# v loaded as fp32 by SyncE's queue and cast on chip, and every engine's order given as a list

## The chip, the cores and the metric

The kernel runs on one core of one Trainium2 chip. A core has five engines that work side by side and meet through semaphores: TensorE (PE, matrix products), VectorE (DVE), ScalarE (ACT), GpSimd (POOL) and SyncE (SP, which here only issues DMAs). Each takes its own instructions strictly in the order in which they were written. The metric is the time on the device in microseconds (us), as the median of some runs; less is better.

## The reference

Two layers follow one another. The first is causal attention with a choice of key chunks: 4 batches, 8 heads, 768 positions, 64 dimensions, 24 chunks of 32 keys. The second is an FFN over the 3072 rows of 512 that attention gives.

```python
k_min, k_max = min and max of k over each chunk of 32 keys
ub = sum over d of maximum(q * k_min, q * k_max)      # an upper bound per query and chunk
top_chunks = the 6 chunks with the largest ub among the causal ones
scores = q @ k.T / 8, masked to the chosen chunks and to keys not after the query
attn = softmax(scores) @ v

rms = sqrt(mean(x * x) + 1e-6);  xn = x / rms * rms_g
out = (silu(xn @ w_gate) * (xn @ w_val)) @ w_out       # 512 -> 1536 -> 512
```

## The kernel before

**Tiling.** Attention goes by pairs of heads: 4 batches of 4 pairs, 16 pairs (p0 to p15), each with 768 positions in 6 tiles of 128. The steps of a pair, by the names that the code gives them: `kload`, `qload` (DMAs into buffers of the kind `nat`, 7 of them, 2 heads side by side); `kT`, `qT` (fp32 transposes on PE, three tiles a step) and `kE`, `qE` (their evictions from PSUM); `kmx`, `kmn`, `dif` (chunk maxima, minima, difference); `kC`, `qC` or `qN` (casts to bf16); `relu`, `ub`, `ubE`, `up`, `ubm` (the bounds: matmul, eviction, transpose, causal mask; for p6 and later two pairs at once, in `duo`); `max`, `sel` (the sixth largest bound and the 0/1 choice), which go to PE's operand through `selT` and `selC` for p0 to p2 and through a DMA transpose on SP (`qX`) from p3 on; `sc`, `exp`, `mask`, `av` (scores, exponential, diagonal mask from batch 1 on, product with v), 6 groups for each of two heads (p3 is worked in two halves of three query tiles); and `xb` (division by the sum).

v of a pair (step `v`, function `load_v`, line 477) is one DMA on GpSimd's queue. It reads fp32 rows of 64 from DRAM and writes bf16 into one of four buffers VX, of 12 x 65 elements a partition, whose column 64 holds ones, set at the start, so that `av` also gives the sum of the exponentials.

The FFN goes by half batches of 384 rows (f0.0 to f3.1). A norm n of the same name comes ahead of each: three `sq` (sums of squares), `eps`, `root`, three `xs` (scaled rows), then a transpose on PE (`tp`, `tpE`) for batch 0 or by DMA on SP (`xT`) later. Then 12 times `gate`, `tanh`, `tg`, `val`, `hh`, and for each of three row tiles three `po` (products with w_out), `poE` (eviction) and `out` (DMA on SP). The weights come as six DMAs of 768 KB on GpSimd's queue (`wg`, `wv`, `wo`).

**Order.** The code first adds all steps to a list, each with its dependencies, the buffers that it opens and uses, the engines that may take it and a planned duration; class `Order` (line 79) then puts them in order. `run` plays the program forward: whenever an engine is free it takes, of the steps that are ready and find buffers, the one with the lowest rank. The ranks are sums of the numbers in `RANK` and `TIMES`. `LIMITS` keeps the 8 PSUM banks apart: so many for scores, preparation, FFN and so on. The steps are then emitted by their planned start. The engine of a step with several choices is the one that takes it first.

**Fillers.** Step `busy` is a matmul on zeros into a free PSUM bank: 48 of 512 columns, free from the start, and 40 of 256 columns, free after the last scores of p2. Their rank is 1000 and more, so the planner takes one only where PE has nothing else.

The lines that the sections below speak of: 346 (filler), 481 (v load), 505 (k and q load), 525 (`kT`, `qT`), 297 to 303 (function `evict`: evictions and casts, whatever the step), 565 (`qX`), 876 (`sc`), 893 (`exp`), 912 (`av`), 932 and 933 (`xb`), 960 and 963 (`sq`), 989 (`xs`), 1045 (`gate`), 1052 (`tanh`), 1058 (`tg`), 1066 (`val`), 1074 (`hh`), 1086 (`po`), 1101 (`out`).

Of the kernel before, what the change touches and what calls it, by code (L numbers as in the profile page):

```python
# [8 lines left out]
FP32 = mybir.dt.float32  # L9
# [16 lines left out]
RANK = (  # L26
    dict(
        av=439.71, dif=-349.0, eps=-276.35, exp=56.9, kC=119.11, kE=221.89, kT=-479.5,
        kload=-91.99, kmn=-561.73, kmx=-221.73, max=-117.69, qC=120.39, qE=644.67, qN=97.14,
        qT=303.27, qX=110.23, qload=17.43, relu=-156.64, root=392.56, sc=392.96, sel=176.91,  # L30
        selC=388.0, selT=-168.59, sq=-325.5, tp=-47.15, tpE=460.17, ub=-387.44, ubE=-1000.64,
        ubm=-238.37, up=-379.03, vload=-360.06, xb=-167.37, xs=293.02,
    ),
    dict(
        av=-243.01, dif=-122.81, eps=-968.41, exp=80.0, gate=-57.45, hh=-33.27, kC=474.21,
        kE=54.78, kT=-28.02, kload=327.35, kmn=571.37, kmx=673.95, mask=-6.85, max=351.72,
        out=-338.93, po=268.25, poE=188.61, qE=-4.14, qN=444.8, qT=271.57, qX=-691.62,
        qload=314.07, relu=202.91, root=-1348.37, sc=-186.72, sel=354.08, sq=285.76, tanh=579.3,
        tg=-259.04, ub=-101.04, ubE=-390.25, ubm=307.49, up=-117.99, val=-52.48, vload=103.56,
        xT=119.23, xb=-299.83, xs=-84.52,  # L40
    ),
)

TIMES = {
# [34 lines left out]
class Order:  # L79
# [18 lines left out]
    def run(self, places):  # L98
        import heapq
        for s in self.steps:  # L100
            s.rank = sum(places[k] * x for k, x in s.keys.items())
            for d in s.deps:
                d.next.append(s)
            s.left = len(s.deps)
        free = {e: 0.0 for e in ("PE", "ACT", "DVE", "POOL", "SP")}
        held = {k: [None] * n for k, n in self.slots.items()}
        count = {}
        waiting = {e: [] for e in free}
        dma = port = 0.0
        n = 0  # L110
        for s in self.steps:
            s.n = n
            n += 1
            if not s.left:
                for e in s.engs:
                    waiting[e].append(s)
        events = [0.0]
        out = []
        while len(out) < len(self.steps):
            if not events:  # L120
                stuck = [x for e in waiting for x in waiting[e] if x.start is None]
                raise RuntimeError("no step can go: " + ", ".join(x.name for x in stuck[:20]))
            t = heapq.heappop(events)
            while events and events[0] <= t + 1e-9:
                heapq.heappop(events)
            for e in free:
                if free[e] > t + 1e-9:
                    continue
                best = None
                for s in waiting[e]:  # L130
                    if s.start is not None or s.ready > t + 1e-9:
                        continue
                    if best is not None and (s.rank, s.n) >= (best.rank, best.n):
                        continue
                    if s.load > 250000 and dma > t + 3.0:
                        heapq.heappush(events, dma - 3.0)
                        continue
                    ok, want = True, {}
                    for b in s.opens:
                        if b.slot is not None:  # L140
                            continue
                        if b.sub and count.get(b.sub, 0) + want.get(b.sub, 0) >= self.limits(b.sub, t):
                            ok = False
                        got = sum(h is None or (h.users == 0 and h.done <= t + 1e-9)
                                  for h in held[b.kind])
                        want[b.kind] = want.get(b.kind, 0) + 1
                        if b.sub:
                            want[b.sub] = want.get(b.sub, 0) + 1
                        if got < want[b.kind]:
                            ok = False  # L150
                    if ok:
                        best = s
                if best is None:
                    continue
                s = best
                s.start, s.eng = t, e
                occ = s.occ[e]
                if e == "PE" and t < self.COLD:
                    occ = 2 * occ

                if e == "DVE" and s.port:
                    occ = max(free["POOL"] - t, 0.0) + occ
                    port = t + occ
                elif e == "POOL":
                    occ = max(port - t, 0.0) + occ
                s.seen = t + occ + self.TAIL[e]
                if s.load:
                    dma = max(dma, t + occ) + s.load / self.RATE
                    s.seen = dma + 1.5
                free[e] = t + occ  # L170
                heapq.heappush(events, free[e])
                heapq.heappush(events, s.seen)
                for b in s.opens:
                    if b.slot is None:

                        b.slot = min((i for i, h in enumerate(held[b.kind])
                                      if h is None or (h.users == 0 and h.done <= t + 1e-9)),
                                     key=lambda i: held[b.kind][i].done if held[b.kind][i] else -1.0)
                        held[b.kind][b.slot] = b
                        if b.sub:  # L180
                            count[b.sub] = count.get(b.sub, 0) + 1
                for b in s.bufs:
                    b.users -= 1
                    b.done = max(b.done, s.seen)
                    if b.users == 0 and b.sub:
                        count[b.sub] -= 1
                for x in s.next:
                    x.left -= 1
                    x.ready = max(x.ready, s.seen)
                    if not x.left:  # L190
                        for y in x.engs:
                            waiting[y].append(x)
                        heapq.heappush(events, x.ready)
                for y in s.engs:
                    waiting[y].remove(s)
                out.append(s)
        self.span = max(s.seen for s in out)
        return out
# [3 lines left out]
def kernel(  # L202
# [11 lines left out]
    nc = tc.nc  # L214
# [22 lines left out]

# [921 lines left out]
```

## Time and profile before

| | us |
|---|---|
| median of 3 runs (315.83 to 316.9) | 315.89 |
| span of the profiled execution | 314.0 |
| PE busy | 308.6 (98%) |
| DVE busy | 230.7 (73%) |
| ACT busy | 194.4 (62%) |
| POOL busy | 100.7 (32%) |

The profiled execution's own time is its span, from the first to the last instruction; the median lies 1.9 us above it. Times in rows are us from the span's start. A row of a group reads: line, engine, operation, output <- input with shapes, count | busy us, mean ns of one | idle time ahead, and what ended it. A row of a window reads: the stretch, its length, busy us and count of instructions of each engine, granted clock of PE, share of the DMA engines, GB/s. A row of a wait reads: who, for whom: us in total, times, longest. A row of the timeline reads: start, duration, engine, line, what, count, and in brackets the idle time ahead. Busy time of PE runs from the first start to the modelled end of pipelined matmuls, so PE can be busy throughout and still have room.

### The profile page before, as it was taken

To read this page: it belongs to the slowest core of one execution; us is meant where nothing else is said; L and a number is where in the kernel's file an instruction comes from. 1 tells how busy PE (TensorE), PEld (TensorE's weight loads), DVE (VectorE), ACT (ScalarE), POOL (GpSimd) and SP (SyncE) were. 2 spreads that over 40 slices of the span, in tenths; PEclk is the share of its full clock that TensorE was granted. 3 is DMA by queue.
4 is the path that set the end of the run, shared out by engine and by line. 5 is a ranking of instruction groups with operands and counts; after the bars stand their busy time and mean duration, and the time that the engine had idled before them with its cause. 6 is when DMAs were issued, how large, how long until landed. Compare 5 with 4: busy or idle time off the path is not lost.

```text
span 314.0 us, 7640 instructions
## 1 busy us (share of the span) xinstructions
PE 308.6 (98%) x2844; PEld 196.1 (62%) x2844; DVE 230.7 (73%) x654; ACT 194.4 (62%) x420; POOL 100.7 (32%) x157
## 2 busy tenths in 40 slices
PE   7999999999999999999999999999999999999995
PEld 4567877666566775666667565656666645655542
DVE  7699986888988487967986799879464663873530
ACT  5589987863475987478579654344988823333321
POOL 8666534342353564045357300001522220000000
PEclk9999999999999999999999999999999999999999
DMA  8999989989989898979934640002341045001102
GB/s 171 210 190 178 145 108 207 198 114 143 196 86 199 126 179 152 201 164 222 158 79 61 93 102 0 2 2 52 84 94 59 20 118 150 3 0 65 38 22 111
DMA packets 113301, 35.36 MB, mean 113 GB/s; under 512 B 106224, under 2 KB 110064, under 8 KB 113264
## 3 DMA queue, kind: packets, MB, share of 16 engines
q1 hardware_dynamic: 83152, 26.62, 40.9%
q0 software_dynamic: 28512, 7.87, 25.6%
q10 hardware_dynamic: 1600, 0.39, 0.6%
q8 instruction: 22, 0.36, 0.5%
q14 instruction: 15, 0.12, 0.1%
HBM read 28.57 MB, written 6.29 MB: 111 GB/s over the span
## 4 chain that ended last, share of the span: by engine, by line
PE 97%; DMA 1%; ACTq 0%; ACT 0%; issue 0%
PE gp L1045 20%; PE vp L1066 20%; PE po L1086 20%; PE sc L876 12%; PE av L912 7%; PE busy L346 4%; PE pq L525 4%; PE pk L525 3%; PE ub L789 2%; PE ub L731 2%; DMA qnat<-in_q_dram 1%; PE up L811 1%; PE sc L882 1%; PE up L755 1%; PE tp L1011 0%; ACTq L505 0%
## 5 line engine op out<-in xcount | busy, mean ns | idle before, releaser
L893 ACT ACTIVATE pt<-sc 128x512 bf16<-128x512 f32 (+2 forms) x192 | 88.4, 578 | 10.1 <-PE sc L876 5.3
L1052 ACT ACTIVATE sg<-gp 128x384 bf16<-128x384 f32 x96 | 47.7, 500 | 62.7 <-PE gp L1045 60.0
L1066 PE MATMUL vp<-xT,wv 128*128 128x384 bf16 x384 | 77.0, 326 | 0.0
L1045 PE MATMUL gp<-xT,wg 128*128 128x384 bf16 x384 | 76.2, 326 | 0.0
L1086 PE MATMUL po<-wo,hh 128*128 128x512 bf16 x288 | 69.3, 379 | 0.0
L1058 DVE SCALAR_TENSOR_TENSOR tg<-sg,gp 128x384 bf16<-128x384 bf16 x96 | 52.2, 548 | 21.7 <-ACT sg L1052 19.5
L1074 DVE TENSOR_TENSOR hh<-vp,tg 128x384 bf16<-128x384 f32 x96 | 51.8, 551 | 11.1 <-PE vp L1066 7.3
L1045 PEld LDWEIGHTS <-wg 128*128 128x128 bf16 x384 | 36.8, 98 | 24.5 <-issue 1.0
L1066 PEld LDWEIGHTS <-wv 128*128 128x128 bf16 x384 | 36.9, 98 | 24.1
L876 PE MATMUL sc<-qs,ke 128*128 128x128 bf16 (+5 forms) x420 | 51.4, 251 | 0.0
L1086 PEld LDWEIGHTS <-hh 128*128 128x128 bf16 x288 | 27.6, 98 | 27.5
L301 POOL CAST ke<-kt 64x768 bf16<-64x768 f32 x31 | 26.4, 852 | 36.9 <-ACT kt L297 17.0
L876 PEld LDWEIGHTS <-ke 128*128 128x128 bf16 (+1 forms) x420 | 30.3, 97 | 11.3 <-issue 1.6
L899 POOL TENSOR_SCALAR_AFFINE_SELECT pt<-pt 128x512 bf16<-128x512 bf16 (+1 forms) x48 | 24.4, 527 | 37.6 <-ACT pt L893 37.4
L912 PEld LDWEIGHTS <-pt 128*128 128x128 bf16 x672 | 28.8, 98 | 7.7 <-POOL ke L301 0.6
L912 PE MATMUL av<-vx,pt 128*128 128x65 bf16 x672 | 32.6, 193 | 0.0
L299 ACT ACTIVATE osb<-po 128x512 f32<-128x512 f32 x19 | 11.4, 602 | 21.4 <-PE po L1086 21.4
L346 PE MATMUL busy<-zeros 128*128 128x512 bf16 (+1 forms) x88 | 20.1, 349 | 1.3 <-DVE zeros L341 1.3
L933 DVE TENSOR_TENSOR xb<-av,rden 128x384 bf16<-128x384 f32 (+1 forms) x34 | 18.1, 534 | 1.2
L989 DVE SCALAR_TENSOR_TENSOR xs<-xb,ri,gains 128x512 bf16<-128x512 bf16 x24 | 16.9, 746 | 2.7 <-DMA xT<-xs 2.1
L301 POOL CAST qn<-qnat 128x768 bf16<-128x768 f32 x10 | 8.2, 821 | 31.9 <-DMA qs<-qn 30.7
L481 POOL DMA_DIRECT2D vx<-in_v_dram x16 | 16.8, 1052 | 4.0 <-PE av L912 2.6
(87 smaller groups left out, 303.1 us busy)
## 6 DMA issues: line engine op xcount, KB each, us to landing
out_dram<-osb SPq DMA_DIRECT2D x24, 256.0 KB, 2.2
knat<-in_k_dram SPq DMA_DIRECT2D x30, 192.0 KB, 4.3
qnat<-in_q_dram SPq DMA_DIRECT2D x30, 192.0 KB, 4.8
vx<-in_v_dram POOLq DMA_DIRECT2D x16, 192.0 KB, 4.7
wg<-in_moe_w_gate_dram POOLq DMA_DIRECT2D x2, 768.0 KB, 8.6
wv<-in_moe_w_val_dram POOLq DMA_DIRECT2D x2, 768.0 KB, 7.8
wo<-in_moe_w_out_dram POOLq DMA_DIRECT2D x2, 768.0 KB, 9.9
qs<-qn SPq DMA_TRANSPOSE x26, 3.3
```

The source lines that it names most:

```text
L301: engine[e].tensor_copy(out_, in_)
L346: nc.tensor.matmul(t[:, 0:n], zeros[:, 0:P], zeros[:, 0:n], start=True, stop=True)
L876: nc.tensor.matmul(t[:, x:x + m, :].rearrange("p a b -> p (a b)"), ke[kk, kb * P:(kb + 1) * P], qs[kk, q0 * P:(q0 + m) * P], start=not tri ...
L893: nc.scalar.activation(out=t[:, 0:nn, :], in_=sc.tile[:, 0:nn, :], func=ACT.Exp, scale=SCALE)
L899: nc.gpsimd.affine_select(out=pt.tile[:, 0:nd, :], in_=pt.tile[:, 0:nd, :], compare_op=ALU.is_ge, fill=0.0, base=0, pattern=[[0, nd], [1, ...
L912: nc.tensor.matmul(av.tile[:, qi - i0, :], pt.tile[:, x, :], VX[c.v.slot][:, hl * NT + kb, :], start=(begin and m == 0), stop=(left[0] == ...
L1045: nc.tensor.matmul(t[:], wg[:, g, hs], XT[b].tile[:, g, cols], start=(g == 0), stop=(g == NP - 1))
L1052: nc.scalar.activation(out=t[:], in_=gp.tile[:], func=ACT.Tanh, scale=0.5)
L1058: nc.vector.scalar_tensor_tensor(out=t[:], in0=sg.tile[:], scalar=1.0, in1=gp.tile[:], op0=ALU.add, op1=ALU.mult)
L1066: nc.tensor.matmul(t[:], wv[:, g, hs], XT[b].tile[:, g, cols], start=(g == 0), stop=(g == NP - 1))
L1074: nc.vector.tensor_tensor(out=t[:], in0=vp.tile[:], in1=tg.tile[:], op=ALU.mult)
L1086: nc.tensor.matmul(po.tile[:], hhs[ht].tile[:, th * P:(th + 1) * P], wo[:, ht, :], start=(ht == 0), stop=(ht == NHT - 1))
```

## The change

1. `VDIRECT = range(16)`: for every pair, `load_v` now makes two steps. `vget` loads v as fp32 by SP's queue into a buffer of the kind `nat`, of which there are 7 as before, now for k, q and v. `vC` casts it on chip into VX, on POOL, DVE or ACT.
2. `RANK`, `TIMES` and the forward planner are gone. `PROGRAM` lists for each engine the numbers of the steps that it takes, in order; `run` only works out when each would start, which buffer it gets, and in which order the instructions are written. The per-use limits on PSUM banks no longer bind. A step that stands in no list isn't emitted: these are 17 of the 48 fillers of 512 columns and all 40 of 256.
3. Loads of k and q in another layout (`three`) are added, and switched off by `K3, Q3 = 0, 0`.

Of the v casts 7 stand in POOL's list (p0, p3, p4, p5, p7, p13, p14), 6 in DVE's (p1, p2, p6, p11, p12, p15) and 3 in ACT's (p8, p9, p10). By the planner before, 19 of the 24 `poE` were on ACT and 5 on DVE; by the lists, 12 and 12.

```diff
-RANK = (
...
-TIMES = {
...
+PROGRAM = {
+    "PE": (
+        "4 5 6 83 89 7 85 8 9 91 10 11 12 13 14 15 16 154 156 103 17 161 159 106 18 19 20 21 22 23 171 111 332 174 "
...
+    "SP": (
+        "81 87 82 88 153 158 70 69 329 334 221 226 113 181 398 74 403 540 249 355 354 356 474 469 545 424 423 559 564 "
...
-    def run(self, places):
...
+    def run(self, program):
+        engines = ("PE", "ACT", "DVE", "POOL", "SP")
+        todo = {e: [self.steps[int(x)] for x in program[e].split()] for e in engines}
...
+        def when(e):
+            if head[e] >= len(todo[e]) or todo[e][head[e]].left:
+                return None
+            s = todo[e][head[e]]
+            t, want = max(free[e], s.ready), {}
+            for b in s.opens:
+                if b.slot is None:
+                    n = want[b.kind] = want.get(b.kind, 0) + 1
+                    if len(slots[b.kind]) < n:
+                        return None
+                    t = max(t, slots[b.kind][n - 1][0])
+            if s.load > 250000:
+                t = max(t, dma - 3.0)
+            return t
...
+    K3, Q3 = 0, 0
+    VDIRECT = range(16)
...
     def load_v(c, lr):
         b, h0 = c.b, c.h0
 
+        if c.p in VDIRECT:
+            vn = Buf("nat")
+
+            def get(e):
+                t = tile_of(vn, [P, 2 * NT, D], FP32, "vnat")
+                nc.sync.dma_start(out=t[:], in_=v[b, h0:h0 + 2].rearrange("h (t p) d -> p (h t) d", p=P))
+
+            x = add("vget", "SP", 1.0, rank(lr, b, "vload"), get, opens=[vn], load=S * 550)
+            c.vload = add("vC", "", {"POOL": pool(2 * NT * D), "DVE": 0.5, "ACT": act(2 * NT * D)},
+                          rank(lr, b, "vload"), lambda e: evict(e, VX[c.v.slot][:, :, 0:D], vn.tile[:]),
+                          [x] + c_vx, opens=[c.v], uses=[vn], port=True)
+            return
+
         def go(e):
...
-    PLACE.update(TIMES)
-
-    done = order.run(PLACE)
+    done = order.run(PROGRAM)
```

The start of SP's list, by name, is: k and q of p0 in alternating halves, k and q of p1, `ke`, k and q of p3, k and q of p2, v of p0, v of p1, k of p4, `gains`, q of p4, k of p6, v of p2, `qX` of p3, v of p3, q and k of p5. Before, `gains` stood ahead of p1. In POOL's list the step behind the cast of p3's v is the first `wg`.

More of the change, by code (lines that the diff above doesn't have):

```diff
@@ L22 @@
 GUARD = 480.0
-RANK = (
[L27 to L32, printed above, removed]
-    ),
[L34 to L40, printed above, removed]
-    ),
-)
-TIMES = {
[15 rows of a table removed]
+PROGRAM = {
[34 rows of a table added]
+    ),
+    "ACT": (
[17 rows of a table added]
+    ),
+    "DVE": (
[20 rows of a table added]
+    ),
+    "POOL": (
[6 rows of a table added]
+    ),
[6 rows of a table added]
+    ),
 }
@@ L96, in add @@
         return s
-    def run(self, places):
-        import heapq
+    def run(self, program):
+        engines = ("PE", "ACT", "DVE", "POOL", "SP")
+        todo = {e: [self.steps[int(x)] for x in program[e].split()] for e in engines}
         for s in self.steps:
-            s.rank = sum(places[k] * x for k, x in s.keys.items())
+            s.left = len(s.deps)
             for d in s.deps:
                 d.next.append(s)
[L104 to L117, printed above, removed]
-        out = []
[L119 to L197, printed above, removed]
@@ new lines, in run @@
+        free = {e: 0.0 for e in engines}
+        slots = {k: [(0.0, i) for i in range(n)] for k, n in self.slots.items()}
+        dma = port = self.span = 0.0
+        head = {e: 0 for e in engines}
+        out = []
+        def when(e):
[12 more added lines that the diff above has]
+            return t
@@ new lines, in run @@
+        total = sum(len(x) for x in todo.values())
+        while len(out) < total:
+            t = e = None
+            for x in engines:
+                y = when(x)
+                if y is not None and (t is None or y < t - 1e-9):
+                    t, e = y, x
+            if t is None:
+                raise RuntimeError("no step can go")
+            s = todo[e][head[e]]
+            head[e] += 1
+            s.start, s.eng = t, e
+            occ = s.occ[e]
+            if e == "PE" and t < self.COLD:
+                occ *= 2
+            if e == "DVE" and s.port:
+                occ = max(free["POOL"] - t, 0.0) + occ
+                port = t + occ
+            elif e == "POOL":
+                occ = max(port - t, 0.0) + occ
+            s.seen = t + occ + self.TAIL[e]
+            if s.load:
+                dma = max(t + occ, dma) + s.load / self.RATE
+                s.seen = dma + 1.5
+            free[e] = t + occ
+            self.span = max(self.span, s.seen)
+            for b in s.opens:
+                if b.slot is None:
+                    b.slot = slots[b.kind].pop(0)[1]
+            for b in s.bufs:
+                b.users -= 1
+                b.done = max(b.done, s.seen)
+                if not b.users:
+                    w = len(slots[b.kind])
+                    while w and slots[b.kind][w - 1][0] > b.done:
+                        w -= 1
+                    slots[b.kind].insert(w, (b.done, b.slot))
+            for x in s.next:
+                x.left -= 1
+                x.ready = max(x.ready, s.seen)
+            out.append(s)
@@ L497, in prep, with load @@
             nat[w], big[w] = Buf("nat"), Buf("qt")
-            def load(e, w=w, src=src, r0=0, rn=nb):
+            three = p < (K3 if w == "k" else Q3)
+            def load(e, w=w, src=src, three=three, r0=0, rn=nb):
+                if three:
+                    if nat[w].tile is None:
+                        tile_of(nat[w], [P, NT // 3, 2, 3 * D], FP32, w + "nat")
+                    for hl in range(2):
+                        eng = nc.scalar if p == 0 and hl else nc.sync
+                        eng.dma_start(out=nat[w].tile[:, r0 // 3:(r0 + rn) // 3, hl, :],
+                                      in_=src[b, h0 + hl, r0 * P:(r0 + rn) * P].rearrange(
+                                          "(g p s) d -> p g (s d)", p=P, s=3))
+                    return
                 if nat[w].tile is None:
@@ L511, in prep @@
                           lambda e, load=load, r0=r0: load(e, r0=r0, rn=3), opens=[nat[w]],
-                          load=3 * P * 550) for r0 in range(0, nb, 3)]
+                          load=3 * P * (380 if three else 550)) for r0 in range(0, nb, 3)]
             else:
                 ld = [add(w + "load", "SP", 1.4, rank(lr, b, w + "load"), load, opens=[nat[w]],
-                          load=n * 550)] * 2
+                          load=n * (380 if three else 550))] * 2
             ready[w] = ld
@@ L527, in turn @@
                             nat[w].tile[:, j0 + j].rearrange("p h d -> p (h d)"), ident_f[:])
-                tr = add(w + "T", "PE", 0.33, rank(at, b, w + "T", j0, "step"), turn, [ld[j0 // 3], c_id],
+                tr = add(w + "T", "PE", 0.83 if three else 0.33, rank(at, b, w + "T", j0, "step"), turn, [ld[j0 // 3], c_id],
                          opens=[bank], uses=[nat[w]])
```

20 lines of the change are left out of this document (14 added, 6 removed), and 94 rows, old and new, of tables (PROGRAM, TIMES).

## The prediction

> **What bounds the kernel now.** I read the page's first part, then the windows by stage, then what PE waited for.
>
> ```profile
> PE 308.6 (98%) x2844; PEld 196.1 (62%) x2844; DVE 230.7 (73%) x654; ACT 194.4 (62%) x420; POOL 100.7 (32%) x157
> ```
> ```profile
> core 0: us, PE busy (x) PEld busy (x) DVE busy (x) ACT busy (x) POOL busy (x), PEclk, DMA share, GB/s
> 0.00:16.00 16.00, 14.41 (x105) 7.66 (x111) 11.42 (x36) 8.66 (x13) 12.04 (x30) 1.00 0.89 190
> 16.00:53.80 37.80, 37.77 (x535) 29.17 (x519) 34.28 (x119) 34.48 (x78) 19.25 (x26) 1.00 1.19 164
> 53.80:309.90 256.10, 256.10 (x2217) 159.29 (x2215) 184.97 (x500) 150.50 (x328) 69.44 (x105) 1.00 0.59 100
> 309.90:314.00 4.10, 0.33 (x2) 0.00 (x0) 0.00 (x0) 0.75 (x2) 0.00 (x0) 1.00 0.34 128
> ```
> ```profile
> PE busy L346 <- DVE zeros L341: 1.3, 1, 1.3
> PE pq L525 <- DMA qnat<-in_q_dram: 0.3, 1, 0.3
> ```
>
> PE never waits after 6 us: 1.3 and 0.3 are all its waits. But part of what it does is no work: line 346 is the filler matmul on zeros. Its windows, and the first gate matmul of the FFN, which comes when batch 0's attention and its norm are through:
>
> ```profile
> 0.00:8.00 8.00, 5.25 (x15) 1.76 (x16) 1.00 0.84 173
> ...
> 40.00:53.80 13.80, 7.06 (x43) 3.60 (x43) 1.00 1.03 161
> 53.80:309.90 256.10, 0.17 (x1) 0.00 (x0) 1.00 0.59 100
> ```
> ```profile
> 53.81 4.06 PE L1045 MATMUL gp<-xT,wg 128*128 128x384 bf16 x24
> ```
>
> So there are two kernels in one. Until 53.8 us PE has spare time (fillers are 5.25 of the first 8 us and 7.06 of the 13.8 before the gate) and the chain attention, norm, gate sets the pace; from 16 us on DVE is busy 34.28 of 37.8 us and ACT 34.48. From 53.8 us to 309.9 us PE is full of real matmuls, with no filler and no wait: 256.1 us that no order can shorten, only begin earlier. The last 4.1 us are the last eviction and the output DMA. The time can fall only by an earlier gate, or by real PE work moved ahead of it.
>
> **The change part by part.** I numbered the steps of the new lists in the order in which the code adds them, and compared with the order in which the old planner puts them out.
>
> The gate. The last scale of batch 0's first half (step xs of n0.0, DVE) stands behind less DVE work than before. Prices:
>
> ```profile
> L301 DVE COPY kt<-pk 128x384 f32<-128x384 f32 x10 | 5.4, 551 | 1.0 <-PE pk L525 1.0
> L301 DVE COPY ubs<-ub 96x256 f32<-96x256 f32 x6 | 2.5, 417 | 3.8 <-PE ub L731 3.7
> L554 DVE TENSOR_REDUCE kmx<-kt 128x24 f32<-128x768 f32 x15 | 14.1, 943 | 0.0
> L301 DVE CAST qn<-qnat 128x768 bf16<-128x768 f32 x3 | 1.9, 646 | 0.0
> L933 DVE TENSOR_TENSOR xb<-av,rden 128x192 bf16<-128x192 f32 x4 | 1.4, 357 | 0.1
> L932 DVE RECIPROCAL rden<-av 128x3 f32<-128x3 f32 x4 | 0.7, 173 | 1.4 <-PE av L912 1.4
> L963 DVE CUSTOM_DVE_ANT_0 junk<-xb 128x512 bf16<-128x512 bf16 x9 | 6.1, 688 | 0.2
> L607 DVE TENSOR_TENSOR ku<-kmx,ku 128x24 f32<-128x24 f32 x5 | 0.9, 189 | 0.1
> L301 DVE COPY qs<-st 64x768 bf16<-64x768 bf16 x4 | 2.2, 555 | 0.1
> L643 DVE TENSOR_SCALAR rt<-qt 128x768 f32<-128x768 f32 x4 | 2.3, 564 | 1.3 <-ACT qt L297 1.1
> ```
>
> Ahead of that step DVE loses, net: two k/q evictions (1.10), three bound evictions (1.25), pair 3's qN cast (0.65), pair 6's kmx (0.94), one difference (0.19), one square sum (0.69), and the two norm-outs of pair 3's second half (2 x (0.357 + 0.173) = 1.06): 5.88. It gains pair 0's selection copy (2 x 0.555 = 1.11), pair 4's relu (0.56) and, from this change, the v casts of pairs 1 and 2. A v cast is 128x768 fp32 to bf16, the shape of the qN cast: 0.65 each, 1.29. Net 5.88 - 2.96 = 2.92 less. DVE instructions overlap a little: the steps listed ahead of the last xs add up to 49.2, the windows show 11.42 + 34.28 = 45.7 to 53.8 us. So 2.92 x 0.93 = 2.7 us. ACT ahead of that norm:
>
> ```profile
> L960 ACT ACTIVATE junk<-xb 128x512 bf16<-128x512 bf16 x15 | 9.3, 624 | 3.3 <-DVE xb L933 3.3
> L960 ACT ACTIVATION_READ_ACCUMULATOR junk<-xb 128x1 f32 x15 | 2.9, 193 | 0.0
> L297 ACT ACTIVATE qs<-st 64x768 bf16<-64x768 bf16 x2 | 1.6, 804 | 0.2 <-PE st L702 0.2
> L641 ACT ACTIVATE rt<-qt 128x768 f32<-128x768 f32 x12 | 10.1, 843 | 1.0 <-DVE qt L301 0.4
> ```
>
> The three squares of n0.1 (3 x 0.82), pair 0's selection copy (2 x 0.804) and two relus (2 x 0.84) go: 5.7; small evictions and one square that come to it take some 2.3 back. That is more than DVE's gain, so DVE decides. Gate: 53.8 - 2.7 = **51.1 us**.
>
> PE work ahead of the gate. The new PE list has both k transposes of pair 5 before the gate, the old one had them behind; all else is the same set. One transpose step costs
>
> ```profile
> 64.73 0.66 PE pk L525 x6
> ```
>
> for the two of six matmuls together: 0.66 us less behind the gate, paid in spare time.
>
> Fillers. 31 steps of 88 are left, all of 512 columns: 17 of that kind and all 40 of 256 columns go. Nothing: they filled waits set by DVE, ACT and loads. If that cover is gone it is idle time in the trace instead, not a shorter one.
>
> The v load. Sixteen issues leave POOL, seven casts come to it; three casts go to ACT, six to DVE:
>
> ```profile
> L481 POOL DMA_DIRECT2D vx<-in_v_dram x16 | 16.8, 1052 | 4.0 <-PE av L912 2.6 <-PE sc L876 0.8 <-issue 0.5
> L301 POOL CAST qn<-qnat 128x768 bf16<-128x768 f32 x10 | 8.2, 821 | 31.9 <-DMA qs<-qn 30.7 <-issue 1.1
> L303 DVE TENSOR_SCALAR osb<-po 128x512 f32<-128x512 f32 x5 | 3.4, 689 | 1.4 <-PE po L1086 1.2
> ```
>
> POOL: 16.8 off, 7 x 0.82 = 5.7 on; it was 32% busy, so zero. ACT: 3 x 0.84 = 2.5, all behind the gate, where it is busy 150 of 256. DVE behind the gate: 4 casts (2.6) and seven more output evictions at 0.689 (4.8), less some of the small steps: about 5.5 on 185 of 256. Zero while PE has work queued; if the cover is gone, 5.5 us. SP: sixteen more issues, hidden while it runs ahead; its price when it doesn't is the second rival below. DMA time: in two windows with v alone on GpSimd's queue, and with k and q on SP's,
>
> ```profile
> q0 software_dynamic: 3104, 0.39, 41.0%
> ```
> ```profile
> q1 hardware_dynamic: 4736, 1.18, 53.7%
> ```
>
> (both 15 us long) two v loads took 6.15 us of all engines, 3.1 each; k and q rows, also 256 B each, 8.06 us for 4736 packets, 2.6 per 1552. So v by SP's queue is 0.5 us cheaper per pair, or, taken from below at no contention, more; I count nothing, since no engine's wait on a v load is seen on the path.
>
> Sum: 314.0 - 2.7 - 0.66 = 310.6 us of span. The median of the runs shown, 315.89, is 1.9 above the profiled span; I add it: **312.5 us**.
>
> Bounds. Earliest gate: the new PE list holds 34.3 us of work (old 33.7 by the same rates) and 31 fillers (6.7) ahead of the gate; with 1.3 us start and the 4.1 us that the old stretch lost to half rate at the start and to hand-offs (53.8 - 1.3 - 33.7 - 14.7 for 88 fillers at full rate), 46.4 us: 307.8 us. Latest without harm behind it: 53.8 as now, 315.2 us.
>
> **The rivals.**
>
> (a) The gate nears its PE bound: 307.8. For it, DVE stood idle for 8 us of the first 53.8 (53.8 - 45.7), and a better order could fill that; against it, its steps ahead of the last xs still add up to 46.3 us, and the first wait for loads.
>
> (b) The gate stays, because of a new chain. Pair 3's v is queued on SP behind pair 3's transposes, which wait for DVE's selection; its cast stands on POOL, and the first load of w_gate behind the cast.
>
> ```profile
> 30.74 2.66 SPq L565 DMA_TRANSPOSE qs<-qn  x2
> ```
> ```profile
> 38.53 0.79 POOL L445 DMA_DIRECT2D wg<-in_moe_w_gate_dram  x1
> ```
> ```profile
> DMA to landing us min/median/max: 6.9/8.6/10.2
> ```
> ```profile
> vx<-in_v_dram POOLq DMA_DIRECT2D x16, 192.0 KB, 4.7
> ```
>
> 30.74 + 2.66, 1.0 for the issue (as the old one's 1052 ns), 4.7 to landing, 0.82 for the cast, give w_gate's issue at about 40.0 and its landing between 47 and 51: just in time for 51.1. Each us by which the selection or the v comes later is a us on the gate; 2.7 late is 315.2, no change.
>
> (c) The clock. Fillers of one shape, first and later:
>
> ```profile
> 1.26 2.74 PE L346 MATMUL busy<-zeros 128*128 128x512 bf16 x6 [1.26 <-DVE zeros L341]
> ```
> ```profile
> 7.15 2.54 PE L346 MATMUL busy<-zeros 128*128 128x512 bf16 x11
> ```
>
> 0.46 us each against 0.23: after idleness PE runs at half rate, though the granted clock reads 1.00. With fillers gone PE may be idle long enough before the gate to fall back. Then the first 24 gate matmuls (3.9 us: 24 of 0.163, by the 4.06 of the row above less the overlap of its last) take twice that: 312.5 + 3.9 = 316.4. Against it, 31 fillers are left, eight of them right before the gate. The Trainium skill, "TensorE: Matmul & The Clock Gate", section "HAM oscillation — how this bites in real kernels", says that idle gaps over some 3.4 us throttle PE; the trace shows the two rates, no run here shows the gap.
>
> (d) Slower: in-order lists stall behind the gate. Matching the lists' numbers, ACT takes an exp or tanh out of PE's order at 92 of 288 places, before at 12; whoever waits there holds all behind it. What one late hand-off is worth:
>
> ```profile
> DVE tg L1058 <- ACT sg L1052: 19.5, 19, 4.5
> ```
>
> 1.0 us each. Today none reaches PE. The gain of 3.4 is used up by three or four that do, and it is slower by over 0.5% (1.6 us, about what a measurement of this kernel can tell from no change) from five or six on; seven give 319.5. For it: DVE's 5.5 us more. Against it: the new lists leave more PE work between a score and its av (median 5.2 us, before 2.2).
>
> **How the numbers follow.** Forecast 0.51, at 308.5 to 314.3; (a) 0.10; (b) 0.14; (c) 0.05; (d) 0.20. Faster is forecast and (a), 0.61; same (b) and (c), 0.19; slower (d), 0.20. The range takes the bound of (a), 307.8, and reaches through (b) and (c) into (d), to 318.0; it leaves out the worse half of (d) and a little of (a).
>
> **What would show it.** The first gate row near 51 us, not 53.8; fillers 31, PE idle before the gate; from there to the last po about 255.4 us without waits on PE. v casts of about 0.65, 0.82 and 0.84 us on DVE, POOL and ACT. Wrong if PE waits on av, gate or po appear behind the gate, if w_gate lands after the last transposed row, or if a gate matmul before 60 us takes twice its time.

## The result, and the profile after

The changed kernel takes 325.21 us (median of 4 runs, 323.46 to 325.68), the kernel before, on the same chip, 315.86. The ratio is 1.0284, 95% interval [1.0252, 1.0316]: slower, where 312.5 us was forecast. The profiled execution took 323.46 us, its span is 321.7. Medians here and below are over all executions of a kernel; the ratios leave out those more than 1.5% above its fastest, which are one of four in the experiment that first moves the loads and three of ten in the one with the v part alone (321.65 to 326.79 us, without a profile).

The windows of the changed kernel, cut where those of before were cut: at the first gate product (now 53.16 us) and at the last product.

```profile
core 0: us, PE busy (x) PEld busy (x) DVE busy (x) ACT busy (x) POOL busy (x), PEclk, DMA share, GB/s
0.00:16.00 16.00, 12.98 (x113) 7.44 (x113) 12.42 (x37) 9.67 (x16) 12.01 (x30) 1.00 1.13 197
16.00:53.10 37.10, 34.37 (x467) 24.83 (x465) 31.88 (x109) 31.68 (x73) 16.88 (x22) 1.00 0.99 173
53.10:317.60 264.50, 258.07 (x2210) 159.05 (x2209) 190.45 (x518) 150.54 (x331) 63.36 (x99) 0.99 0.55 107
317.60:321.70 4.10, 0.33 (x2) 0.00 (x0) 0.00 (x0) 0.74 (x2) 0.00 (x0) 1.00 0.34 128
```

The front is 0.65 us shorter. The stretch from the gate to the last product, 256.1 us of unbroken work before, is 264.5 long and PE is busy 258.07 of it. So nearly the whole loss lies behind the gate. What PE waits for (who, for whom: us in total, times, longest), from its largest wait on:

```profile
PE sc L936 <- DMA qs<-qn: 5.8, 1, 5.8
PE busy L371 <- DVE zeros L366: 2.2, 1, 2.2
PE tp L1071 <- DVE xs L1049: 1.0, 1, 1.0
PE pq L581 <- DMA qnat<-in_q_dram: 1.0, 1, 1.0
```

One wait of 5.8 us for a DMA stands out; the others in this list lie ahead of the gate. PE's timeline has the place (start, duration, line, what, count, idle time ahead):

```profile
53.16 2.11 PE L1105 MATMUL gp<-xT,wg 128*128 128x384 bf16 x12
55.15 0.82 PE L1126 MATMUL vp<-xT,wv 128*128 128x384 bf16 x4
...
57.11 0.81 PE L1105 MATMUL gp<-xT,wg 128*128 128x384 bf16 x4
63.73 1.86 PE L936 MATMUL sc<-qs,ke 89*128 89x128 bf16 x8 [5.80 <-DMA qs<-qn]
```

After seven tiles of f0.0, PE's list has p4's first score product. Its operand comes through p4's two `qX` steps, the DMA transposes on SP. Windows of two microseconds of PE alone show what follows (stretch, length, busy us and count, granted clock, DMA share, GB/s):

```profile
58.00:60.00 2.00, 0.00 (x0) 1.00 1.08 133
60.00:62.00 2.00, 0.00 (x0) 0.53 1.52 102
62.00:64.00 2.00, 0.27 (x4) 0.50 1.27 121
64.00:66.00 2.00, 2.00 (x9) 0.50 1.35 217
66.00:68.00 2.00, 2.00 (x13) 0.76 1.35 218
68.00:70.00 2.00, 1.96 (x21) 1.00 1.36 219
```

The granted clock falls to half while PE stands idle and comes back only near 67 us: from 63.73 on that costs, by an estimate from these windows, 0.27 x 0.5 + 2 x 0.5 + 2 x 0.24 = 1.6 us. So 5.8 + 1.6 of the 8.4 us by which that stretch grew sit in this one place.

Why the transposes were late: their issue on SP and the two weight loads on POOL, and then the DMA view of the stretch 47 to 53 us (issues, KB, median us from issue to landing).

```profile
46.94 0.82 POOL L326 CAST qn<-qnat 128x768 bf16<-128x768 f32 x1 [3.44 <-DMA qnat<-in_q_dram]
47.71 0.78 POOL L470 DMA_DIRECT2D wv<-in_moe_w_val_dram  x1
48.51 0.91 POOL L1041 TENSOR_TENSOR ri<-ms,mhalf 128x3 f32<-128x3 f32 x1
...
50.25 0.80 POOL L470 DMA_DIRECT2D wg<-in_moe_w_gate_dram  x1
...
48.63 3.14 SPq L625 DMA_TRANSPOSE qs<-qn  x2
```
```profile
wv<-in_moe_w_val_dram POOLq DMA_DIRECT2D x1, 768.0 KB, 7.4
wg<-in_moe_w_gate_dram POOLq DMA_DIRECT2D x1, 768.0 KB, 13.0
qs<-qn SPq DMA_TRANSPOSE x2, 11.4
```

In the kernel before, the two loads, the issue of the two transposes, and their landing from the view of their tile:

```profile
44.61 0.74 POOL L445 DMA_DIRECT2D wv<-in_moe_w_val_dram  x1
...
49.24 0.80 POOL L445 DMA_DIRECT2D wg<-in_moe_w_gate_dram  x1
```
```profile
45.81 3.44 SPq L565 DMA_TRANSPOSE qs<-qn  x2
```
```profile
DMA to landing us min/median/max: 6.0/6.5/7.0
```

Now the same row reads 9.1/11.4/13.7, where the median over all 26 such transposes is 3.0. They are issued 2.8 us later, and land 3 to 7 us later after that. A load of 768 KB was issued just ahead of them and another between the second one's issue and its landing. Before, the first load went out 1.2 us ahead of the first transpose and the second 1.6 us behind the second (at 47.6), with both transposes issued but not yet landed; now these are 0.9 us ahead and about 0.35 us behind. Two theories were put to the test: that the weight loads beside the transposes make the wait, because all use the same DMA engines ("shared-DMA"), and that the later issue alone does. A third, from the forecast, was that many small waits add up. The runs can show that a load beside a transpose delays it; which part of the path they share, they do not show.

### The profile page after: what moved, and what is told of

The parts are those of the page before. It is cut to its first block, busy times and chain, and to the rows that moved or that the text cites. A ratio compares the mean times of both kernels' runs of the same rounds, so it can differ in the third digit from the quotient of the medians.

```text
span 321.7 us, 7439 instructions
## 1 busy us (share of the span) xinstructions
PE 305.7 (95%) x2787; PEld 191.3 (59%) x2787; DVE 234.8 (73%) x661; ACT 192.6 (60%) x420; POOL 92.2 (29%) x150
## 4 chain that ended last, share of the span: by engine, by line
PE 82%; DMA 6%; DVE 5%; ACT 4%; issue 1%; SPq 1%; POOL 0%; DVEq 0%; POOLq 0%
PE po L1146 19%; PE gp L1105 18%; PE vp L1126 17%; PE sc L936 10%; PE av L972 5%; DMA qs<-qn 4%; PE pk L581 3%; PE pq L581 3%; ACT pt L953 2%; PE ub L849 2%; DMA xT<-xs 2%; PE busy L371 1%; PE ub L791 1%; PE up L871 1%; DVE m L718 1%
## 5 line engine op out<-in xcount | busy, mean ns | idle before, releaser
L953 ACT ACTIVATE pt<-sc 128x512 bf16<-128x512 f32 (+1 forms) x192 | 94.5, 553 | 29.3 <-PE sc L936 28.2
L1112 ACT ACTIVATE sg<-gp 128x384 bf16<-128x384 f32 x96 | 45.7, 493 | 52.0 <-PE gp L1105 48.9
L1126 PE MATMUL vp<-xT,wv 128*128 128x384 bf16 x384 | 74.6, 326 | 0.0
L936 PE MATMUL sc<-qs,ke 128*128 128x128 bf16 (+5 forms) x420 | 58.3, 253 | 6.2 <-DMA qs<-qn 5.8
L972 PEld LDWEIGHTS <-pt 128*128 128x128 bf16 x672 | 34.1, 98 | 12.0 <-ACT pt L953 2.1
L972 PE MATMUL av<-vx,pt 128*128 128x65 bf16 x672 | 40.7, 193 | 0.2 <-ACT pt L953 0.2
L328 DVE TENSOR_SCALAR osb<-po 128x512 f32<-128x512 f32 x12 | 8.3, 692 | 14.6 <-PE po L1146 14.0
L322 ACT ACTIVATE qt<-pq 128x384 f32<-128x384 f32 x25 | 12.2, 495 | 9.6 <-PE pq L581 7.9
L324 ACT ACTIVATE osb<-po 128x512 f32<-128x512 f32 x12 | 7.1, 599 | 18.0 <-PE po L1146 18.0
L581 PE MATMUL pq<-ident_f,qnat 128*128 128x128 f32 x96 | 16.2, 282 | 1.0 <-DMA qnat<-in_q_dram 1.0
```

The source lines that it names most:

```text
L581: nc.tensor.transpose(t[:, j * P:(j + 1) * P], nat[w].tile[:, j0 + j].rearrange("p h d -> p (h d)"), ident_f[:])
L936: nc.tensor.matmul(t[:, x:x + m, :].rearrange("p a b -> p (a b)"), ke[kk, kb * P:(kb + 1) * P], qs[kk, q0 * P:(q0 + m) * P], start=not tri ...
L953: nc.scalar.activation(out=t[:, 0:nn, :], in_=sc.tile[:, 0:nn, :], func=ACT.Exp, scale=SCALE)
L972: nc.tensor.matmul(av.tile[:, qi - i0, :], pt.tile[:, x, :], VX[c.v.slot][:, hl * NT + kb, :], start=(begin and m == 0), stop=(left[0] == ...
L1112: nc.scalar.activation(out=t[:], in_=gp.tile[:], func=ACT.Tanh, scale=0.5)
L1126: nc.tensor.matmul(t[:], wv[:, g, hs], XT[b].tile[:, g, cols], start=(g == 0), stop=(g == NP - 1))
```

## The experiments

All edits are to the changed kernel unless the text says otherwise; lists are given by the names of the steps. The runs were spread over several chips, on which the kernel before took 315.84 to 316.24 us. A table of what the profiles show stands at the end.

**The changed kernel again.**

> The changed kernel, nothing edited, as a measure of its own spread beside the mend on one chip. If the one wait makes the loss, its profile shows that wait again at p4's first score product (5 to 7 us) with the transposes landing 9 us or more after their issue, whatever the first gate product's time is (53 to 55 us), and the time is 322 to 327. If the wait was a chance of the one profile, it is under 3 us here.

Measured: 323.03 us, ratio 1.0211 [1.0146, 1.0276]. The first gate product came at 52.07, and the wait was there again:

```profile
61.91 1.86 PE L936 MATMUL sc<-qs,ke 89*128 89x128 bf16 x8 [4.88 <-DMA qs<-qn]
```

So the wait is no accident of one profile. The time of this kernel moves by some 2 us from one set of runs to the next, which bounds what a single time below can say.

**Leave the second load out.**

```diff
-POOL: ... n0.0.root p4.kC1 wg1 n0.1.root ...
+POOL: ... n0.0.root p4.kC1 n0.1.root ...
-nc.tensor.matmul(t[:], wg[:, g, hs], ...)   # gate tiles 6 to 11
+nc.tensor.matmul(t[:], wg[:, g, gs], ...)   # gs: the columns of tiles 0 to 5
```

> Left out: the load of the second half of the gate weights; gate tiles 6 to 11 read the first half's columns instead, so those outputs are other numbers. All lists are the changed kernel's. Shared-DMA theory (p4's two query transposes, issued at 48.6 and 49.9 us, land 9.1 and 13.7 us later because the weight loads of 47.7 and 50.3 us are read beside them): the landing falls to 6 to 8 us, TensorE's 5.8 us wait at p4's first score product falls to 0 to 2, the half-rate stretch behind it goes, and the time falls by 5 to 8 us, to 317 to 320. Late-start theory (the transposes are issued 2.8 us later than before, and that alone makes the wait): the landing stays at 9 to 14 us and the time within 1 us of the changed kernel's 325.2. Many-small-waits theory (the in-order lists lose time everywhere): likewise no more than 1 us.

Measured: 317.61 us, 1.004 [1.0026, 1.0055]. No wait at the score product, granted clock 1.00 throughout, 261.2 us from the gate to the end of the span (268.5 in the changed kernel). The transposes, issued at 50.2 and 51.5, later still than in the changed kernel, landed thus:

```profile
DMA to landing us min/median/max: 6.2/6.4/6.6
```

This takes the late-start theory away as a cause by itself: the start was 1.5 us later and the wait was gone. One load, the value weights at 48.45, still ran beside them.

**Put work in the wait.** Two edits that leave the DMAs alone: four ready tiles ahead of the score products, or seventeen fillers.

```diff
-PE: ... gate3 p4.sc0.0.0 p4.sc0.0.3 p4.sc1.0.2 p4.sc0.0.4 gate0 val3 ... val5 p4.sc0.0.5 val0 p4.sc1.0.4 ...
+PE: ... gate3 gate0 val3 ... val5 val0 p4.sc0.0.0 p4.sc0.0.3 p4.sc1.0.2 p4.sc0.0.4 p4.sc0.0.5 p4.sc1.0.4 ...
```

> On TensorE's list p4's first five score products stand behind four more gate and value tiles of the first FFN group, and ScalarE's list has that tanh ahead of the exponentials. The DMAs are untouched. If one wait, that for p4's query transposes, makes the loss, some 2.6 us of ready matmuls now run inside it: the time falls by 2.6 to 4 us, to 321 to 322.6, and the wait at the score product shrinks from 5.8 to about 3. Many-small-waits theory: a change of under 1 us, and the time lost turns up at other hand-offs.

Measured: 321.9 us, 1.0166 [1.0136, 1.0196]; the wait is 3.0, landing 11.3 to 12.7. Forecast 2.6 to 4 less, found 3.3 less than the first run of the changed kernel and 1.1 less than the second. The wait shrank from 5.8 or 4.9 to 3.0, by 1.9 to 2.8 where some 2.6 us of work was put into it, which the many-small-waits theory has no place for.

```diff
-PE: ... gate3 p4.sc0.0.0 ...
+PE: ... gate3 busy x17 p4.sc0.0.0 ...
```

> Seventeen filler products stand on TensorE's list right ahead of p4's first score product, where the changed kernel idles 5.8 us. The DMAs are untouched, so p4's transposes land as late as before and the score product starts within 1 us of 63.7. Clock theory (the idle stretch costs twice: first 5.8 us of waiting, then a stretch at a lower granted clock): the half-rate stretch behind the wait is gone, the granted clock is 1.00 throughout, and the time falls by 1.3 to 2 us, to 323.2 to 324. If the low clock is only a mark and not a cost: within 0.5 us of 325.2.

Measured: 321.82 us, 1.0178 [1.0129, 1.0227]. The landing was late as ever (12.8 to 13.2), 1.95 us of waiting stayed behind the fillers, and the granted clock fell all the same:

```profile
64.00:66.00 2.00, 1.52 (x12) 0.99 1.35 217
66.00:68.00 2.00, 2.00 (x11) 0.50 1.36 218
68.00:70.00 2.00, 2.00 (x10) 0.66 1.35 217
```

The expectation of a full clock was wrong. From gate to end it is 267.8 us, 0.7 less than in the changed kernel. The time is below both times of the changed kernel, by 3.4 and 1.2 us, and its runs (319.39 to 323.46) overlap those of the second. What the half rate costs was not isolated; 1.6 us stays a number worked out from the windows.

**Move the loads.** First only the order on POOL, so that the cast of p6's queries no longer holds up what stands behind it:

```diff
-POOL: ... p6.qN wv0 n0.0.root p4.kC1 wg1 n0.1.root ...
+POOL: ... wv0 n0.0.root p4.kC1 p6.qN wg1 n0.1.root ...
```

> On GpSimd's list the cast of p6's queries, which waited 3.44 us for its load, stands behind the first value-weight load and the first norm's root instead of ahead of both. Everything else is the changed kernel's. Expected: the value weights are issued some 4 us sooner (about 43.5 us) and the root at about 46.6, so the first gate product comes 1.5 to 2 us sooner, at about 51.5. Shared-DMA theory: with those weights nearly landed when p4's transposes are issued, their landing falls from 9.1 and 13.7 to 7 to 10 us, and the time falls by 3 to 6 us. Late-start theory: the transposes are issued at the same 48.6 us and land as late, so p4's scores start at the same 63.7 us, the sooner gate is swallowed by a longer wait, and the time stays within 0.5 us of 325.2.

Measured: 321.16 us, 1.013 [1.0081, 1.0179]. The value weights went out at 44.48, 3.2 us sooner where 4 were expected, but the gate came no sooner: 53.16. The root now ended at 48.47, and the scaled rows waited on DVE for p4's selection instead. The two transposes fell apart:

```profile
DMA to landing us min/median/max: 2.5/5.9/9.3
```

The second gate-weight load was issued at 50.82, between the two (49.7 and 51.0). The wait at the score product was 2.5 us.

With that load also behind the second norm's root:

```diff
-POOL: ... wv0 n0.0.root p4.kC1 p6.qN wg1 n0.1.root ...
+POOL: ... wv0 n0.0.root p4.kC1 p6.qN n0.1.root wg1 ...
```

> As the kernel with the p6 cast moved, and the second half of the gate weights is issued behind the second norm's root, some 5 us later, when p4's transposes should have landed. Shared-DMA theory: the transposes land 6 to 7 us after their issue, the wait at p4's first score product is at most 2 us; but the gate weights land near 66 us, and a wait of 2 to 4 us for them stands at the first gate tile that reads them, so the time is 317 to 321. Late-start theory: the wait at the score product keeps 4 us or more and the new one comes on top, 325 or more.

Measured: 321.05 us, 1.0155 [1.0138, 1.0171]. Both transposes landed 3.0 and 3.5 us after their issue and the wait at the score product was gone; the load, at 59.23, was now too late:

```profile
PE gp L1114 <- DMA wg<-in_moe_w_gate_dram: 2.1, 1, 2.1
PE pq L590 <- DMA qnat<-in_q_dram: 1.8, 1, 1.8
```

(PE's waits between 44 and 75 us.) The second of these lies ahead of the gate, so one wait had been traded for another; the time missed the expected 317 to 321 by a little.

Then three mends with the load in between, alike but for what the load waits for. In all three PE's two transposes of p6's queries, and their evictions on ACT, stand behind the first gate tiles.

```diff
 POOL: ... wv0 n0.0.root p4.kC1 p6.qN wg1 n0.1.root ...
+c_w[1][0].deps.append(c.sel[1])      # first mend: in the plan, the first transpose
+c_w[1][0].deps += c.sel              # second mend: in the plan, both
+nc.gpsimd.tensor_copy(mark[:, hl:hl + 1], QS[...][hl][0:1, 0:1])   # third: read both tiles, then load
```

> A mend by the shared-DMA theory, the full change kept: on GpSimd's list the first value weights and the norm's root stand ahead of p6's query cast, and the second half of the gate weights waits until the first of p4's two query transposes has landed (about 53 us). TensorE's two transposes of p6's queries stand behind the first gate tiles. Expected: p4's transposes land 3 to 6 us after their issue, no wait of over 1 us at the score product, the first gate product at 51 to 52 us, at most 1.5 us of waiting for the late gate weights, and a time of 313 to 316.5. If the loss has another root than those transposes, it stays at 319 or more.

> As the mend before it, with one difference: the second half of the gate weights waits for both of p4's query transposes, not for the first alone (there the first landed 2.5 us after its issue and the second, with the weights beside it, 9.5). Shared-DMA theory: both land 2.5 to 4 us after their issue, no wait over 0.5 us at the score product; the gate weights are issued at about 55.5 and a wait of 0 to 2.5 us stands at the first gate tile that reads them; from the first gate product to the end it takes 261 to 263.5 us (263.9 with the first alone), and the time is 317 to 319.5. If the second transpose was late for another reason (SyncE's queue, its own size): it still takes 8 us or more and the time stays at 320.

> The mend with a real wait: ahead of the load of the second half of the gate weights GpSimd copies one element out of each of the two tiles that p4's transposes write, so that it reaches the load only when both have landed (in the two mends before, the wait was an entry of the plan alone, and the chip issued the load at 52.6 to 52.8, between the two transposes). Shared-DMA theory: both transposes land 2.5 to 4 us after their issue, no wait over 0.5 us at p4's first score product; the weights are issued at 54.5 to 57 us, a wait of 0 to 2.5 us stands at the first gate tile that reads them; 261 to 263.5 us from the first gate product to the end (263.9 and 264.3 in the two mends), time 317 to 319.5. If the second transpose was late for another reason: it still takes 8 us or more, and the time stays at 320 to 321.

Measured: 320.17 us (1.0131 [1.011, 1.0153]), 320.99 (1.0146 [1.0118, 1.0174]) and 318.13 (1.0053 [1.0029, 1.0078]). The first two expectations rested on a wait that the chip never made: in this kernel a dependency added to the plan orders the plan alone. POOL issued the load when it got there, at 52.78 and 52.58. The first mend's rows, POOL's timeline and then the view of the tile that the transposes write (durations in ns, first and last start in us), are the clearest sight of the cause that the study has:

```profile
51.53 1.31 POOL L329 CAST qn<-qnat 128x768 bf16<-128x768 f32 x1
52.78 0.80 POOL L473 DMA_DIRECT2D wg<-in_moe_w_gate_dram  x1
```
```profile
L628 SPq DMA_TRANSPOSE qs<-qn x2: 1273/1280/1287, 51.7 to 53.0; - x2
DMA to landing us min/median/max: 2.5/6.0/9.5
```

The transpose issued 1.1 us ahead of the load takes 2.5 us, the one issued 0.2 us behind it 9.5, and a wait of 2.2 us stayed at the score product. The second mend repeats it (2.9 and 9.2, a wait of 1.8), and so did the kernel with only p6's cast moved (2.5 and 9.3). The third has the real wait, and differs from the second in nothing else (timeline, then landing):

```profile
54.91 0.97 POOL L476 COPY mark<-qs 1x1 bf16<-1x1 bf16 x2 [3.01 <-DMA qs<-qn]
55.83 0.81 POOL L477 DMA_DIRECT2D wg<-in_moe_w_gate_dram  x1
```
```profile
DMA to landing us min/median/max: 2.5/2.7/2.9
```

No wait at the score product, none for the weights, granted clock 0.998 over the span, 262.3 us from gate to end instead of 264.3. The full change, with p6's cast and transposes moved and one wait added, is 4.9 us faster than the changed kernel's second set of runs (taken on the same chip) and 7.1 than its first, and still 0.5% slower than the kernel before. From gate to end it takes 2.1 us more than before: up to the last product PE is idle for 1.4 of it, 0.94 in one wait for a step `hh` on DVE at 151.32, and busy 0.8 longer.

**The two parts apart.** The order without the v part, and the v part without the order.

```diff
-VDIRECT = range(16)
+VDIRECT = ()            # v by GpSimd's queue; in the new POOL list at places that the plan chose
```

> The order part alone: the new lists, but v of all pairs read and cast by GpSimd's queue as in the kernel before, each v load set into GpSimd's list at the place that the plan found best, and the casts of v dropped from the lists. If the order makes the loss (it puts weight loads beside p4's transposes), this kernel shows a wait of 2 us or more for those transposes and is slower than before, 318 to 325. If the v part makes it (twice the bytes of v, and its wait ahead of the weights on GpSimd), there is no such wait and the time is 312 to 316.

Measured: 330.9 us, 1.047 [1.0423, 1.0517]. PE's largest waits:

```profile
PE sc L939 <- DMA qs<-qn: 6.8, 3, 5.6
PE av L975 <- DMA vx<-in_v_dram: 4.0, 2, 3.4
```

The same wait, 5.6 us at its longest, with no v on SP's queue at all; the 4.0 us for v come from the places chosen here, so the time is no price of the order alone.

```diff
-PROGRAM = {...}
+PROGRAM = {...}   # the order of the kernel before, with the loads and casts of v set in
```

> The v part alone: the order is the kernel before's, step for step on every engine, written as lists; v is read as fp32 by SyncE's queue, and its casts are set into GpSimd's, VectorE's and ScalarE's lists where the plan found room. If the order makes the loss: no wait for p4's transposes of over 1 us, and the time within 1.5 us of before, 314.5 to 317.5. If the v part makes it: such a wait of 3 us or more, or one of that size at another load, and 319 or more.

Measured: 317.01 us, 1.0031 [1.0016, 1.0045]. No wait on PE over 0.4 us behind its first product, 260.7 us from gate to end (260.2 before). The transposes landed 8.1 and 9.4 us after an issue at 45.8 and 47.1: later than before, with the two loads where they had been (44.71 and 49.34), so the v part slows these transposes too, by 2.1 to 2.4 us; no one waited. By the ratio the v part costs about 1 us; what in it does so was not found.

**The conflict without the lateness.** On the kernel before:

```diff
-POOL: ... wv0 n0.0.root wg1 n0.1.root ...
+POOL: ... wv0 wg1 n0.0.root n0.1.root ...
```

> The kernel before, step for step, with one step moved: the second half of the gate weights stands on GpSimd's list ahead of the first norm's root instead of behind it, so that it is issued at about 45.4 us, beside p4's transposes (45.8 and 47.6, used at 57.7), and not at 49.2. Nothing is late here. Shared-DMA theory: the transposes land 9 to 13 us after their issue instead of 6.0 and 7.0, at 56 to 60.5, and a wait of 0.5 to 3 us stands at p4's first score product; the time is 316.5 to 320. Late-start theory: they were issued in time, the landing is of no account, and the time stays within 0.5 us of before.

Measured: 316.4 us, 1.0008 [0.9999, 1.0018]. Issue of the load, and landing of the transposes:

```profile
45.60 0.75 POOL L474 DMA_DIRECT2D wg<-in_moe_w_gate_dram  x1
```
```profile
DMA to landing us min/median/max: 10.9/11.3/11.7
```

Half right. The load beside them took the landing of the transposes from 6.0 and 7.0 us to 10.9 and 11.7, as the shared-DMA theory says. But they were issued at 46.1 and 47.7, and PE came to p4's scores at 58.19 without a wait. The time is what the late-start theory said: the slack of the old order paid for the slower landing.

| kernel | gate at | transposes to landing | wait at the score | gate to end | median |
|---|---|---|---|---|---|
| before | 53.81 | 6.0, 7.0 | none | 260.2 | 315.86 |
| changed | 53.16 | 9.1, 13.7 | 5.8 | 268.5 | 325.21 |
| changed, again | 52.07 | 8.3, 12.0 | 4.9 | 269.3 | 323.03 |
| without the second load | 53.90 | 6.2, 6.6 | none | 261.2 | 317.61 |
| third mend | 54.18 | 2.5, 2.9 | none | 262.3 | 318.13 |
| v part alone | 53.98 | 8.1, 9.4 | none | 260.7 | 317.01 |
| before, load moved | 54.28 | 10.9, 11.7 | none | 260.3 | 316.4 |

What follows: in these runs the wait came only with both. Late transposes with one load fewer beside them (the kernel without the second load) and slow transposes issued early (the kernel before with its load moved) brought no wait at the score product; the new order has them late and slow. No version tried here beats the kernel before.

## Why the prediction was wrong

**The step that failed** is the one that called the stretch behind the gate "256.1 us that no order can shorten, only begin earlier". The sum took 255.4 us for it, without a wait; measured to the last product it is 264.5. An order can lengthen it, and this one did, by one wait of 5.8 us for a DMA and the half rate behind it. DMAs were counted there by queue (sixteen more issues on SP, "hidden while it runs ahead") and by the total of the v loads; which loads run beside which transposes was not worked out. The step moved without being priced was p4's selection. On DVE it now stands behind the first norm's sum `ms`; before and now:

```profile
43.44 0.99 DVE L658 MAX8 m<-ubm 128x8 f32<-128x8 f32 x12
```
```profile
46.22 0.17 DVE L1033 TENSOR_SCALAR ms<-ss 128x3 f32<-128x3 f32 x1 [0.36 <-ACT junk L1020]
46.30 0.99 DVE L718 MAX8 m<-ubm 128x8 f32<-128x8 f32 x12
```

So its transposes go out 2.8 us later (48.63, before 45.81), and the weight loads moved towards them. The excess over the forecast, 325.2 - 312.5 = 12.7 us, divides by profile rows into 9.0 behind the gate (268.5 against 310.6 - 51.1 = 259.5), of which 5.8 is the wait, about 1.6 the half rate and the rest is not attributed; 2.1 for the gate (53.16 against 51.1); and 1.6 because the profiled execution was the fastest of the four (median 3.5 above its span, where 1.9 was added).

**The gate, 51.1.** Measured 53.16 and 52.07. The instructions that the prediction counted off DVE did go. But up to the end of the three scaled rows (52.20 before, 52.17 now) DVE's busy time fell only from 44.14 to 43.42 us, not by 2.7, since others took longer: the scaled rows 2.7 us instead of 2.1, the selections of p3 and p4 (`qn`) 2.5 instead of 1.3. And DVE does not seem to set the gate alone. The chain that the profile gives ends in p4's transposes, but its pieces up to `ms` lead to the first norm as well; from 16 us on they are 17.8 us of PE, 8.1 of ACT and 3.4 of DVE. The last two:

```profile
44.85 1.35 ACT junk L1020 x4
...
46.22 0.17 DVE ms L1033
```

`ms` of the first norm ended at 46.39, 1.85 us sooner than before; then POOL stood at p6's cast, which waited 3.44 us for its load, with the value weights and the root behind it, and the lead was gone: the root ended at 49.42, before at 49.27. Moving the cast did not bring the gate forward, since DVE's selection of p4 then stood ahead of the scaled rows. The gate also moves from run to run: with the changed kernel's lists up to there it came at 52.07 to 54.07, with p6's cast moved at 53.16 to 55.10. In all ten profiles it follows the first load of the gate weights by 15.1 to 15.8 us, so the spread arises ahead of that load, which is issued between 36.34 and 39.45. What makes it stays open, and so the 2.1 us are not a price of the lists alone.

**What held, in part.** Without the half rate's 1.6 us, PE's 258.07 us of work behind the gate are 256.5 (255.4 forecast), so the 0.66 us of p5's transposes moved ahead can't be made out. The casts of v came at 0.55 us on DVE and 0.86 on POOL and ACT, near the 0.65, 0.82 and 0.84 of the forecast, and PE's listed waits behind the gate (5.8 and 0.4 us) are both for DMAs and not for a late cast.

**The rivals.** (a), the gate at its PE bound, did not come. (d) had the right sign and the wrong mechanism: not five to seven hand-offs between engines at 1 us, but one wait for a DMA. In the changed kernel's profile no list of ACT or DVE held PE behind the gate; in other profiles with these lists single hand-offs did, for 0.5 to 1.0 us each, but never the five to seven of (d). (c), the clock, came true behind the wait and not at the gate. (b) named the chain over p3's v and POOL to the gate weights; POOL did wait 6.44 us for that v, the load went out at 37.33, and it arrived in time.

## What to carry to other kernels

Before a reordering is priced, list for each DMA on the path what is issued within some 10 us of it on any queue: here a transpose took 2.5 us when it went out 1.1 us ahead of a 768 KB load and 9.5 us when it came 0.2 us behind it. Issue early the transfers that PE will wait for, and let big loads with slack wait for them by a true data dependency; in this kernel an entry in the plan was no wait. A stretch without waits can rest on slack in its transfers, and an order can use that slack up without a sign in the time (the kernel before with its load moved) until it is gone.

## What the runs showed that was not expected

Transposes of one size landed after 2.5 to 13.7 us, by what was in flight with them. The Trainium skill, "Trainium Kernel Development and Optimization", section "Key Constraints", says that DMAs of the SP, ACT and POOL queues run on the same 16 engines and interleave. The rows above fit that, and give the price: in three profiles a transpose issued 1.1 us ahead of a 768 KB load of another queue landed after 2.5 to 2.9 us, its twin 0.1 to 0.2 us behind the load after 9.2 to 9.5.

Idle time and the granted clock: waits of 5.80, 5.59, 4.88, 3.41, 3.0, 2.51, 2.08 and 1.95 us were each followed by a stretch at half rate, waits of 2.18 and 1.80 us were not. The Trainium skill, "TensorE: Matmul & The Clock Gate", section "HAM oscillation — how this bites in real kernels", speaks of gaps over some 3.4 us; here four clearly shorter ones had it too, so the length alone does not decide. After the waits of 3.0, 2.51 and 1.95 us the clock fell only 1.2 to 1.5 us after PE was at work again. What else decides was not tested.
